# The first gate weights moved to SyncE's queue, and tile 1's statistics split around the first square root

## Chip, cores, metric

One core of a Trainium2 chip. The metric is the device time of the slowest (here the only) core in microseconds (us).

## The reference

```python
# x: (1, 2048, 512) bf16; F = 1376; all dims of the state space model are 512
xn = layernorm(x)                                     # per row, no affine part
# branch A: h[t] = Lam_bar * h[t-1] + B_bar @ xn[t]   (complex, diagonal Lam_bar)
#           y[t] = 2 * Re(C @ h[t]) + xn[t] * Dskip
# branch B: (silu(xn @ w_gate) * (xn @ w_up)) @ w_down
return x + A(xn) + B(xn)
```

## The kernel before: what matters here

x is cut into 16 tiles of 128 rows, four of them a chunk. Chunk 0 is on the path from the start: its tiles are normalized, transposed by TensorE and multiplied with the gate weights, one tile ("quarter") at a time. Later chunks are transposed by DMA. A list scheduler in the kernel orders the work of VectorE, ScalarE and GpSimd from estimated durations; TensorE's and SyncE's orders are as written.

The loads, all in SyncE's queue but two:

```python
x_load(0)
x_load(1)
act_q = [dma("ld_touch", tch[0:16, 0:1], wg_v[0:128:8, 0:1, 0:2], ..., eng="act")]   # 64 bytes
act_q.append(wg_load("a0", 0, 2, eng="act", order=(act_q[-1],)))    # gate weights, K tiles 0 and 1
x_load(2)
wg_load("a1", 2, 3)                                                 # K tile 2
wg_load("a2", 3, 4)                                                 # K tile 3
x_load(3)
pload("ld_ldt", 2, A_log_dt); pload("ld_lim", 1, A_Lambda_im); pload("ld_lre", 0, A_Lambda_re)
dma("ld_wu0", ...)      # up weights, 768 KB
dma("ld_wg1", ...)      # the other gate weights, 480 KB
dma("ld_wu1", ...)      # the other up weights, 608 KB
dma("ld_x4", ...)       # x tiles 4 to 7, 512 KB
# then, each behind all before it: transposing loads of B_re, B_im (needed by the first
# matmul of the state space branch), xT of chunk 1, x8-11, C_re, C_im, Dskip, x12-15, ...
```

VectorE's order for tiles 0 to 3 ("b": statistics of half a tile, "B": of a whole one, "s": aggregate, after which ScalarE takes the square root, "r": reciprocal, "n": normalize):

```python
last = ln_stat0(0, (bn_full(0),))
for op, a, h in (("r", 0, 0), ("n", 0, 0), ("B", 1, 0), ("s", 1, 0), ("b", 2, 0),
                 ("r", 1, 0), ("n", 1, 0), ("n", 1, 1), ("b", 2, 1), ("s", 2, 0), ...
```

Of the kernel before, what the change touches and what calls it, by code (L numbers as in the profile page):

```python
# [249 lines left out]
def bass_parallel_sum__ssm_conv_s5__swiglu_ffn__prompt_kernel(  # L250
# [30 lines left out]
    g = _Graph()  # L281
    es = ExitStack()
    with es:
        block = es.enter_context(nc.Block(no_gpsimd_drain=True))

        def sb(name, shape, dt):
            return es.enter_context(nc.sbuf_tensor(name, shape, dt))
# [39 lines left out]
        mv = sb("mv", [128, NT, 2], F32)  # L327
# [5 lines left out]
        st0 = st[:].rearrange("p (a h) s -> p a h s", h=2)  # L333
# [62 lines left out]
        def dma(name, dst, src, writes, nbytes, reads=(), after=(), out_=False, eng="sp", xpose=False, prio=0.0, order=(), **kw):  # L396
            after = tuple(after)
            if xpose:
                after = after + tuple(dma_tasks)
                fn = lambda e, dst=dst, src=src: e.dma_start_transpose(out=dst, in_=src)  # L400
                est, nb = 1900.0, int(nbytes * 1.2) + 140000
            else:
                if xp_state[0] is not None:
                    after = after + (xp_state[0],)
                fn = lambda e, dst=dst, src=src: e.dma_start(dst, src, **kw)  # L405
                est, nb = 330.0 + nbytes / 900.0, nbytes
            t = g.add(eng, fn, reads=reads, writes=writes, name=name, dma=True, after=after, out=out_, est=est, nbytes=nb, prio=prio, order=order)
            dma_tasks.append(t)
            if xpose:
                xp_state[0] = t  # L410
            return t
# [9 lines left out]
        def x_load(a, **kw):  # L421
            return dma("ld_x%d" % a, x_sb[:, a:a + 1, :], x_v[:, a:a + 1, :], [("x", a)], TILEB, **kw)

        def wg_load(nm, k0, k1, **kw):
            return dma("ld_wg" + nm, wg[:, k0:k1, 0:FG], wg_v[:, k0:k1, 0:FG], [("wg", nm)], (k1 - k0) * 128 * FG * 2, **kw)
# [2 lines left out]
        x_load(0)  # L428
        x_load(1)
        act_q = [dma("ld_touch", tch[0:16, 0:1], wg_v[0:128:8, 0:1, 0:2], [("tch",)], 16 * 4, eng="act")]  # L430
        act_q.append(wg_load("a0", 0, 2, eng="act", order=(act_q[-1],)))
        x_load(2)
        wg_load("a1", 2, 3)
        wg_load("a2", 3, 4)
# [13 lines left out]
        def loads_stage_b2():  # L448
# [11 lines left out]
              reads=[("dsk",)], writes=[("ident",)], name="ident", est=300)  # L460
        g.add("pool", lambda e: e.iota(iot[:], pattern=[[1, TP]], base=0, channel_multiplier=0, allow_small_or_imprecise_dtypes=True),
              writes=[("iot",)], name="iota", est=1000)
# [49 lines left out]
        def bn_half(a, h, order=()):  # L512
            return g.add("dve", lambda e: e.bn_stats(out=st0[:, a, h, :], in_=x_sb[:, a, h * 256:(h + 1) * 256]),
                         reads=[("x", a)], writes=[("st0", a, h)], name="bnst%d_%d" % (a, h), est=350, order=order)

        def ln_half(a, h, order=()):
            cs = slice(0, 384) if a == 0 else slice(h * 256, (h + 1) * 256)
            return g.add("dve", lambda e: e.tensor_scalar(out=xn_sb[:, a % NXN, cs], in0=x_sb[:, a, cs], scalar1=mv[:, a, 0:1], scalar2=rstd[:, a:a + 1],
                                                        op0=ALU.subtract, op1=ALU.mult),
                         reads=[("x", a), ("mv", a), ("rstd", a)], writes=[("xh", a, h)], name="xn%d_%d" % (a, h), est=300, order=order)  # L520

        def ln_stat0(a, order):
            t = g.add("dve", lambda e: e.bn_aggr(out=mv[:, a, :], in_=st0[:, a].rearrange("p h s -> p (h s)")[:, 0:6 if a < 2 else 12]),
                      reads=[("st0", a, h) for h in range(1 if a < 2 else 2)], writes=[("mv", a)], name="bnag%d" % a, est=160, order=order)
            hold["sd%d" % a] = g.add("act", lambda e: e.activation(out=sd0[:, a:a + 1], in_=mv[:, a, 1:2], func=AF.Sqrt, bias=epst[:, 0:1]),
                                     reads=[("mv", a), ("epst",)], writes=[("sd0", a)], name="sd%d" % a, est=280)
            return t

        def ln_chunk0():
            def bn_full(a, order=()):  # L530
                return g.add("dve", lambda e: e.bn_stats(out=st0[:, a, 0, :], in_=x_sb[:, a, :]), reads=[("x", a)], writes=[("st0", a, 0)], name="bnst%d" % a, est=640, order=order)
            def recip(a, order):
                return g.add("dve", lambda e: e.reciprocal(out=rstd[:, a:a + 1], in_=sd0[:, a:a + 1]), reads=[("sd0", a)], writes=[("rstd", a)],
                             name="rstd%d" % a, est=140, order=order)
            last = ln_stat0(0, (bn_full(0),))
            g.add("act", lambda e: e.activation(out=nm0[:, 0:1], in_=mv[:, 0, 0:1], func=AF.Identity, scale=-1.0), reads=[("mv", 0)], writes=[("nm0", 0)],
                  name="negm0", est=220, order=(hold["sd0"],))
            hold["negm0"] = g.tasks[-1]
            for op, a, h in (("r", 0, 0), ("n", 0, 0), ("B", 1, 0), ("s", 1, 0), ("b", 2, 0),
                             ("r", 1, 0), ("n", 1, 0), ("n", 1, 1), ("b", 2, 1), ("s", 2, 0), ("b", 3, 0),  # L540
                             ("r", 2, 0), ("n", 2, 0), ("n", 2, 1), ("b", 3, 1), ("s", 3, 0), ("p", 0, 0),
                             ("r", 3, 0), ("n", 3, 0), ("n", 3, 1)):
                if op == "r":
                    last = recip(a, (last,))
                    if a == 0:
                        g.add("act", lambda e: e.activation(out=nm0[:, 1:2], in_=nm0[:, 0:1], func=AF.Identity, scale=rstd[:, 0:1]),
                              reads=[("nm0", 0), ("rstd", 0)], writes=[("nm0", 1)], name="nmr0", est=290)
                        hold["nmr0"] = g.tasks[-1]
                        g.add("act", lambda e: e.activation(out=xn_sb[:, 0, 384:512], in_=x_sb[:, 0, 384:512], func=AF.Identity, bias=nm0[:, 1:2], scale=rstd[:, 0:1]),
                              reads=[("x", 0), ("rstd", 0), ("nm0", 1)], writes=[("xh", 0, 1)], name="xn0_1", est=400)  # L550
                        hold["xa01"] = g.tasks[-1]
                elif op == "n":
                    last = ln_half(a, h, (last,))
                elif op == "b":
                    last = bn_half(a, h, (last,))
                elif op == "B":
                    last = bn_full(a, (last,))
                elif op == "p":
                    last = g.add("dve", lambda e: e.transpose(out=prT[:], in_=prow[:]), reads=[("prow", k) for k in range(3)] + [("prow0",)],
                                 writes=[("praw", k) for k in range(3)], name="parT", est=90, order=(last,))  # L560
                else:
                    last = ln_stat0(a, (last,))
            hold["xn3"] = last
# [220 lines left out]
        def ffn_gate_quarters(pairs):  # L784
# [5 lines left out]
            pe_warm(9, 512, wbank)  # L790
            pe_warm(2, 128, wbank)
            ln_chunk0()
            xt_tile_fine(0, 0, wbank)
            pe_warm(1, 256, tiles[-2][1])
# [305 lines left out]
```

## Time and profile before

| | before |
|---|---|
| time, median of the first 3 runs | 178.72 us (178.62 to 178.73) |
| profiled execution | 179.2 us, span 177.4 us |
| TensorE busy | 173.9 us (98% of the span) |
| VectorE, ScalarE busy | 92%, 49% |

In lines of the profile, PE is TensorE, PEld its weight loads, DVE VectorE, ACT ScalarE, POOL GpSimd; SPq and ACTq are the issuing of DMAs by SyncE and ScalarE. L405 is a line of the kernel, x14 the number of instructions merged into the line, and times are in us. A K tile is 128 of the 512 rows of a weight matrix; xT is a transposed x.

The chain that ended last, by engines, from the page of before:

```profile
PE 62%; DMA 19%; DVE 7%; ACT 4%; SPq 3%; POOL 1%; issue 1%; ACTq 0%
```

A kernel whose TensorE is busy 98% has a last chain that runs through DMAs for its first third. So two chains are nearly level there.

SyncE's issues in the timeline of before (start, duration, what). The load of K tiles 0 and 1 is not here: ScalarE issued it at 1.23.

```profile
0.79 1.34 SPq L405 DMA_DIRECT2D x_sb<-in_A_x_dram  x3
2.18 0.91 SPq L405 DMA_DIRECT2D wg<-in_B_w_gate_dram  x2
3.13 0.43 SPq L405 DMA_DIRECT2D x_sb<-in_A_x_dram  x1
...
5.52 0.44 SPq L405 DMA_DIRECT2D wu<-in_B_w_up_dram  x1
...
7.10 0.82 SPq L405 DMA_DIRECT2D x_sb<-in_A_x_dram  x1
16.58 2.02 SPq L400 DMA_TRANSPOSE BT<-in_A_B_re_dram  x1
20.78 1.78 SPq L400 DMA_TRANSPOSE BT<-in_A_B_im_dram  x1
24.77 2.86 SPq L400 DMA_TRANSPOSE xnT<-xn_sb  x1
```

A transposing load is issued when all before it have landed. So the last three lines also tell landings: x4-7 by 16.58, B_re by 20.78, B_im by 24.77 (the landing records have 16.28, 20.77 and 24.70).

VectorE's first work in the timeline of before. In brackets is idle time and what ended it.

```profile
3.67 0.18 DVE L523 BATCH_NORM_AGGREGATE mv<-st 128x2 f32<-128x6 f32 x1
4.21 0.16 DVE L533 RECIPROCAL rstd<-sd 128x1 f32<-128x1 f32 x1 [0.36 <-ACT sd L525]
4.41 0.38 DVE L518 TENSOR_SCALAR xn_sb<-x_sb,mv,rstd 128x384 bf16<-128x384 bf16 x1
4.71 0.69 DVE L531 BATCH_NORM_STATS2 st<-x_sb 128x6 f32<-128x512 bf16 x1
5.43 0.18 DVE L523 BATCH_NORM_AGGREGATE mv<-st 128x2 f32<-128x6 f32 x1
5.53 0.40 DVE L513 BATCH_NORM_STATS2 st<-x_sb 128x6 f32<-128x256 bf16 x1
5.97 0.16 DVE L533 RECIPROCAL rstd<-sd 128x1 f32<-128x1 f32 x1
```

TensorE's weight loads before: in the first stage, and at the first matmuls of the state space branch.

```profile
5.50 0.79 PEld L806 LDWEIGHTS pb<-xnT,wg 128*128 128x128 bf16 x14
6.55 0.18 PEld L806 LDWEIGHTS pb<-xnT,wg 128*128 128x128 bf16 x3 [0.26 <-issue]
...
23.73 0.74 PEld L883 LDWEIGHTS pb<-xnT,BT 128*128 128x128 bf16 x4
24.75 0.16 PEld L883 LDWEIGHTS pb<-xnT,BT 128*128 128x128 bf16 x2 [0.27 <-DMA BT<-in_A_B_im_dram]
```

The 0.26 us is read as the wait for K tile 2 (landed 6.45, 0.10 before the gap ends; the profile prints only "issue"). The 0.27 us before the load at 24.75 costs nearly nothing, since weight loads run ahead of the matmuls.

Two matmul lines before: the first 512-wide one, which ends the first stage, and the wait for the last transposed x.

```profile
12.72 1.03 PE L762 MATMUL pb<-xnT,wg 128*128 128x512 bf16 x4
...
64.85 1.04 PE L845 MATMUL pb<-xnT,wg 128*128 128x512 bf16 x4 [0.17 <-DMA xnT<-xn_sb]
```

What the DMAs did meanwhile, in two-microsecond windows of before (length; busy time and count of TensorE, its weight loads, VectorE, ScalarE and GpSimd; granted clock, DMA share, GB/s):

```profile
2.00:4.00 2.00, 2.00 (x6) 0.73 (x5) 0.88 (x2) 1.40 (x3) 0.15 (x3) 1.00 0.98 296
6.00:8.00 2.00, 1.88 (x35) 1.74 (x33) 1.85 (x8) 0.94 (x5) 0.00 (x0) 1.00 0.85 164
14.00:16.00 2.00, 2.00 (x11) 0.92 (x10) 0.00 (x0) 2.00 (x4) 0.00 (x0) 1.00 0.12 35
```

### The profile page before, as it was taken

How to read it: one execution, taken by the hardware profiler on the slowest of the kernel's cores; microseconds unless marked ns; L12 is line 12 of the kernel's file. 1: busy time of each engine (PE TensorE's matmuls, PEld its weight loads, DVE VectorE, ACT ScalarE, POOL GpSimd, SP SyncE). 2: the span in 40 equal slices, each digit the busy share in tenths (PEclk: the TensorE clock that was granted, in tenths of full speed). 3: DMA queues.
4: the chain of work that ended last, by engine and by line, in shares of the span. 5: the costliest groups of instructions: out<-in, count | busy, mean ns of one | idle time of the engine just before them, and what ended most of it. 6: DMA issues, size and time to landing. Idle time of an engine off the chain costs nothing.

```text
span 177.4 us, 2425 instructions
## 1 busy us (share of the span) xinstructions
PE 173.9 (98%) x935; PEld 83.8 (47%) x935; DVE 162.5 (92%) x283; ACT 86.9 (49%) x116; POOL 11.1 (6%) x22
## 2 busy tenths in 40 slices
PE   8999999999999999999999999999999999999994
PEld 2894444444444434444444444444444444444644
DVE  2964999899899999999999999999999999999943
ACT  4679889979978869240456554000265520000000
POOL 3040500050050000000000000000000000000000
PEclk9999999999999999999999999999999999999999
DMA  5992595563468150001100000001100000000032
GB/s 169 268 373 68 120 148 95 161 133 82 134 133 283 29 102 0 0 4 66 54 0 0 0 0 4 0 0 59 59 0 4 0 0 0 0 0 30 32 110 67
DMA packets 22966, 12.37 MB, mean 70 GB/s; under 512 B 15180, under 2 KB 22956, under 8 KB 22956
## 3 DMA queue, kind: packets, MB, share of 16 engines
q1 hardware_dynamic: 22652, 11.77, 24.9%
q10 hardware_dynamic: 304, 0.46, 0.8%
q8 instruction: 7, 0.11, 0.3%
q14 instruction: 3, 0.02, 0.0%
HBM read 6.46 MB, written 2.10 MB: 48 GB/s over the span
## 4 chain that ended last, share of the span: by engine, by line
PE 62%; DMA 19%; DVE 7%; ACT 4%; SPq 3%; POOL 1%; issue 1%; ACTq 0%
PE pb L966 20%; PE pb L762 19%; PE pb L980 16%; DMA x_sb<-in_A_x_dram 7%; DMA xnT<-xn_sb 5%; PE pb L883 4%; SPq L405 3%; DVE st L483 3%; DMA hss<-in_A_C_im_dram 3%; DMA hss<-in_A_C_re_dram 2%; DMA dsk<-in_A_Dskip_dram 2%; PE pb L977 2%; ACT xn_sb L507 2%; DVE hT L834 1%; PE pb L855 1%
## 5 line engine op out<-in xcount | busy, mean ns | idle before, releaser
L923 DVE TENSOR_TENSOR_SCAN rot<-sm,car,rot 128x512 bf16<-128x512 f32 x32 | 38.8, 1266 | 0.0
L774 ACT ACTIVATE sg<-pb 128x1024 bf16<-128x1024 f32 x20 | 20.1, 1023 | 32.1 <-PE pb L762 31.3
L966 PE MATMUL pb<-wd,hT 128*128 128x512 bf16 (+2 forms) x180 | 35.2, 355 | 0.0
L980 PE MATMUL pb<-W,hss 128*128 128x512 bf16 (+2 forms) x144 | 30.3, 355 | 0.0
L762 PE MATMUL pb<-xnT,wu 128*128 128x512 bf16 x120 | 27.9, 379 | 0.0
L966 PEld LDWEIGHTS pb<-wd,hT 128*128 128x128 bf16 x180 | 16.8, 98 | 18.2 <-ACT scrC L730 0.4
L832 ACT ACTIVATE uf<-pb 128x1024 bf16<-128x1024 f32 x20 | 20.5, 1024 | 8.9 <-PE pb L762 7.3
L762 PE MATMUL pb<-xnT,wg 128*128 128x512 bf16 x92 | 21.8, 379 | 0.0
L883 PE MATMUL pb<-xnT,BT 128*128 128x512 bf16 x96 | 21.0, 379 | 0.0
L980 PEld LDWEIGHTS pb<-W,hss 128*128 128x128 bf16 x144 | 13.5, 97 | 14.4
L762 PEld LDWEIGHTS pb<-xnT,wu 128*128 128x128 bf16 x120 | 11.7, 98 | 14.2 <-ACT sg L774 0.2
L890 ACT ACTIVATE u_sb<-pb 128x1024 bf16<-128x1024 f32 x16 | 16.0, 1022 | 3.3 <-PE pb L883 3.3
L883 PEld LDWEIGHTS pb<-xnT,BT 128*128 128x128 bf16 x96 | 9.3, 98 | 11.4 <-DMA BT<-in_A_B_im_dram 0.3
L985 DVE TENSOR_TENSOR x_sb<-pb,x_sb 128x512 bf16<-128x512 f32 (+2 forms) x18 | 11.1, 628 | 3.3 <-PE pb L980 3.0
L762 PEld LDWEIGHTS pb<-xnT,wg 128*128 128x128 bf16 x92 | 9.0, 98 | 10.6
L834 DVE TENSOR_TENSOR hT<-sg,uf 128x1024 bf16<-128x1024 bf16 x20 | 13.4, 681 | 0.4 <-ACT uf L832 0.4
L483 DVE BATCH_NORM_STATS2 st<-x_sb 128x6 f32<-128x512 bf16 x12 | 7.4, 679 | 3.1 <-DMA x_sb<-in_A_x_dram 3.1
L914 DVE TENSOR_TENSOR rot<-u_sb,cosT 128x2048 bf16<-128x2048 bf16 x8 | 9.7, 1218 | 0.0
L914 DVE TENSOR_TENSOR rot<-rot,sin 128x2048 bf16<-128x2048 bf16 x8 | 9.7, 1218 | 0.0
L914 DVE TENSOR_TENSOR rot<-u_sb,sin 128x2048 bf16<-128x2048 bf16 x8 | 9.7, 1218 | 0.0
L914 DVE TENSOR_TENSOR rot<-rot,cosT 128x2048 bf16<-128x2048 bf16 x8 | 9.7, 1213 | 0.0
L914 DVE TENSOR_TENSOR rot<-rot 128x2048 bf16<-128x2048 bf16 x8 | 9.6, 1218 | 0.0
(93 smaller groups left out, 180.4 us busy)
## 6 DMA issues: line engine op xcount, KB each, us to landing
out_dram<-x_sb SPq DMA_DIRECT2D x15, 128.0 KB, 1.7
x_sb<-in_A_x_dram SPq DMA_DIRECT2D x3, 512.0 KB, 4.7
wd<-in_B_w_down_dram SPq DMA_DIRECT2D x1, 1280.0 KB, 8.6
wu<-in_B_w_up_dram SPq DMA_DIRECT2D x1, 768.0 KB, 5.0
wu<-in_B_w_up_dram SPq DMA_DIRECT2D x1, 608.0 KB, 7.0
x_sb<-in_A_x_dram SPq DMA_DIRECT2D x4, 128.0 KB, 3.2
wg<-in_B_w_gate_dram SPq DMA_DIRECT2D x1, 480.0 KB, 5.9
wg<-in_B_w_gate_dram ACTq DMA_DIRECT2D x1, 448.0 KB, 3.8
```

Source lines behind the costliest of these rows:

```text
L483: return g.add("dve", lambda e, a=a: e.bn_stats(out=st[:, a % 8, :], in_=x_sb[:, a, :]), reads=[("x", a)], writes=[("st", a % 8), ("st0", ...
L762: inst = e.matmul(pbank[0:fs, bk, :].rearrange("p (j t) -> p j t", j=4), lhsT=w[:, kt, i * 128:i * 128 + fs], rhs=xnT[c][:, :, kt, :], sta ...
L774: g.add("act", lambda e: e.activation(out=sg[rows, sl, 0:n, :].rearrange("p a t -> p (a t)"), in_=pair_f32(rows, bk, 512 * n), func=AF.Sil ...
L832: g.add("act", lambda e: e.activation(out=uf[rows, ul, 0:n, :].rearrange("p a t -> p (a t)"), in_=pair_f32(rows, bk, 512 * n), func=AF.Ide ...
L834: g.add("dve", lambda e: e.tensor_tensor(out=hT[rows, hb, i0:i0 + n, :], in0=sg[rows, sl, 0:n, :], in1=uf[rows, ul, 0:n, :], op=ALU.mult), ...
L883: inst = e.matmul(pbank[:, bk, :].rearrange("p (j t) -> p j t", j=4), lhsT=BT[:, ri, kt, pt * 128:(pt + 1) * 128], rhs=xnT[c][:, :, kt, :] ...
L890: g.add("act", lambda e: e.activation(out=u_sb[:, us].rearrange("p r t -> p (r t)"), in_=pair_f32(slice(0, 128), b0), func=AF.Identity), r ...
L914: tt = lambda out, a, b, op, r, w, nm: g.add("dve", lambda e: e.tensor_tensor(out=out, in0=a, in1=b, op=op), reads=r, writes=w, name="%s_% ...
L923: g.add("dve", lambda e, A0=A0, A1=A1, k=k, ri=ri, pt=pt: e.tensor_tensor_scan(out=A1[:, k, ri, :], data0=rr[:, pt:pt + 1].to_broadcast([1 ...
L966: inst = e.matmul(pbank[:, bk, 0:nc_], lhsT=hT[0:fs, hb, i, lt * 128:(lt + 1) * 128], rhs=wd[0:fs, i, c0:c0 + nc_], start=(i == 0), stop=F ...
L980: inst = e.matmul(pbank[:, bk, 0:nc_], lhsT=hss[:, hb, pt, ri, lt * 128:(lt + 1) * 128], rhs=W12[:, ri, pt, c0:c0 + nc_], start=False, sto ...
L985: g.add("dve", lambda e, bk=bk, a=a, c0=c0, nc_=nc_: e.tensor_tensor(out=x_sb[:, a, c0:c0 + nc_], in0=pbank[:, bk, 0:nc_], in1=x_sb[:, a, ...
```

## The change

The intent: in one queue the first loads land in the order of need (x0, x1, gate weights, x2, ...), and VectorE uses the 0.36 us in which it waits for the first square root to read half of tile 1.

```diff
         act_q = [dma("ld_touch", ...)]
-        act_q.append(wg_load("a0", 0, 2, eng="act", order=(act_q[-1],)))
+        wg_load("a0", 0, 2)
         x_load(2)
 ...
-            t = ... bn_aggr(... [:, 0:6 if a < 2 else 12]),  reads=[("st0", a, h) for h in range(1 if a < 2 else 2)]
+            t = ... bn_aggr(... [:, 0:6 if a == 0 else 12]), reads=[("st0", a, 0), ("st0", a, 1)]
 ...
-            for op, a, h in (("r", 0, 0), ("n", 0, 0), ("B", 1, 0), ("s", 1, 0), ("b", 2, 0),
+            for op, a, h in (("b", 1, 0), ("r", 0, 0), ("n", 0, 0), ("b", 1, 1), ("s", 1, 0), ("b", 2, 0),
```

A third part isn't in the diff: the scheduler, given other estimates, puts the work on the sine and cosine tables (from 17 us on) in another order on VectorE and ScalarE.

More of the change, by code (lines that the diff above doesn't have):

```diff
@@ L522, in ln_stat0 @@
         def ln_stat0(a, order):
-            t = g.add("dve", lambda e: e.bn_aggr(out=mv[:, a, :], in_=st0[:, a].rearrange("p h s -> p (h s)")[:, 0:6 if a < 2 else 12]),
-                      reads=[("st0", a, h) for h in range(1 if a < 2 else 2)], writes=[("mv", a)], name="bnag%d" % a, est=160, order=order)
+            t = g.add("dve", lambda e: e.bn_aggr(out=mv[:, a, :], in_=st0[:, a].rearrange("p h s -> p (h s)")[:, 0:6 if a == 0 else 12]),
+                      reads=[("st0", a, 0), ("st0", a, 1)], writes=[("mv", a)], name="bnag%d" % a, est=160, order=order)
             hold["sd%d" % a] = g.add("act", lambda e: e.activation(out=sd0[:, a:a + 1], in_=mv[:, a, 1:2], func=AF.Sqrt, bias=epst[:, 0:1]),
@@ L555, in ln_chunk0 @@
                     last = bn_half(a, h, (last,))
-                elif op == "B":
-                    last = bn_full(a, (last,))
                 elif op == "p":
```

## The prediction

> What bounds the kernel now. The page's first part shows TensorE busy 173.9 of 177.4 us; the timeline shows it without a real gap from its first useful matmul (5.52 us) on, except 0.26 us in its weight loads at 6.3 us (the landing times say why: the gate weights of K tile 2 landed at 6.45) and 0.17 us at 64.7 us, waiting for tile-chunk 3's transposed x. The chain of waits names a second limit: SyncE issues its first loads (about 0.47 us each, to 7.10 us), x4-7 land at 16.28, then DMA transposes and loads each wait for the one before: B_re 16.58 to 20.77, B_im to 24.70, xT, x8, C_re, C_im, Dskip, ..., the last xT at 64.81, which releases TensorE for its last 110 us. B_im's landing at 24.70 also ends a 0.27 us weight-load wait just as TensorE needs it. So both chains are level, and a gain counts only if both have it.
>
> What the change does. (1) The 448 KB of gate weights leave ScalarE's queue (issue 1.23, landed 5.03) and become SyncE's third load. The Trainium skill, "DMA: Bandwidth & Descriptors", section "Issuing engines are not separate DMA queues", says that issuing from several engines saves only the sequencer's issue time. Here that time is the point: every later SyncE load is issued about 0.47 us later (wu0 at 5.99, not 5.52; x4-7 at 7.57). (2) In one queue the early loads land in order of need: I expect x1 by about 3.5 (was 4.09), the first gate weights about 4.5 to 4.8 (5.03), K tile 2 under 6.2 (6.45). (3) VectorE reads tile 1's first half (0.40 us) in the idle 0.36 us before the first reciprocal. The reciprocal stays near 4.21; tile 1's aggregate goes from 5.43 to about 5.2, its square root from 5.65 to about 5.5. (4) VectorE's and ScalarE's table work is reordered by the list scheduler; TensorE's order is unchanged.
>
> Costs. TensorE's start (5.5) waits for the evacuation of tile 0's transposes, not for weights, and stays. It loses the 0.26 us gap, and tile 1 is early enough to follow: about 0.25 us gained by 12.7 us (first 512-wide matmul about 12.45). Against that: before, the data of the first loads ended at 6.4 us and the first 1536-byte packets of wu0 started at 6.62, with the DMA engines 3 to 7 of 16 busy in between; so wu0 is bound by its issue there. Issued 0.47 later, wu0, wg1, wu1 and x4-7 land 0.3 to 0.5 later: x4-7 about 16.7, B_re about 21.2, B_im about 25.1. TensorE reaches B_im early, waits, and is about 0.4 us later than before from there on; the last xT lands about 65.2. The reordered table work has slack (PSUM pairs come free over 3 us before their next use).
>
> Predicted 179.1 us, 8 in 10 within 178.6 to 179.5. Chance of faster by over 2%: 0.01; within 2%: 0.98; slower: 0.01.
>
> What would show it: step 1, SyncE's issue times; step 2, landings; step 3, the gap at 6.3 gone, first 512-wide matmul near 12.45; the cost, wu0's first packets near 7.1, x4-7 landing near 16.7, B_im near 25.1, a longer weight-load wait there, last xT near 65.2.
>
> What would make it wrong: wu0's slow first microsecond (6.6 to 8.2) has another cause than its issue and does not move, so that x4-7 land at 16.3 and the time is 178.6 or less; the DMA engine that lands last for x4-7 (1.3 us after the other 15; a 16 KB packet of the instruction queue held one for 0.96 us) falls otherwise; or the reordering makes TensorE wait.

## The result

| | before | changed |
|---|---|---|
| median us, beside each other | 178.76 (178.62 to 179.18, 6 runs) | 179.16 (178.84 to 179.6, 6 runs) |
| ratio, 95% interval | | 1.0019 (1.0003 to 1.0035) |
| span of the profiled execution | 177.4 us | 177.1 us |

A ratio is the mean time of one kernel's fast runs over that of the other's of the same rounds, so not quite the ratio of the medians quoted.

The predicted 179.1 us is met. But the trace at hand is of the fastest of the six executions, and that of before is of one as slow as the slowest of the six beside it (179.2), so the two traces differ the other way round: the changed kernel's span is the shorter. Reading the difference from this pair would be a mistake; what they do show are the steps.

The chain that ended last, from the page of the changed kernel. It is TensorE's alone now:

```profile
PE 96%; ACT 2%; issue 1%; DVE 0%
```

SyncE's issues, changed:

```profile
0.79 0.87 SPq L405 DMA_DIRECT2D x_sb<-in_A_x_dram  x2
1.71 0.43 SPq L405 DMA_DIRECT2D wg<-in_B_w_gate_dram  x1
2.18 0.47 SPq L405 DMA_DIRECT2D x_sb<-in_A_x_dram  x1
...
6.02 0.45 SPq L405 DMA_DIRECT2D wu<-in_B_w_up_dram  x1
...
7.60 0.96 SPq L405 DMA_DIRECT2D x_sb<-in_A_x_dram  x1
16.32 2.00 SPq L400 DMA_TRANSPOSE BT<-in_A_B_re_dram  x1
20.50 1.85 SPq L400 DMA_TRANSPOSE BT<-in_A_B_im_dram  x1
24.69 3.00 SPq L400 DMA_TRANSPOSE xnT<-xn_sb  x1
```

All from wu0 on is issued 0.50 us later. In this execution x4-7 land at the same time all the same. Their last DMA engine is probably the one that also fetched a 16 KB packet of the instruction queue (0.96 us long before, 1.11 here): that is read from the times, since the trace does not number the engines. It lands 1.3 us after the other fifteen before (14.94 and 16.28), and 1.0 us here (15.22 and 16.25). The fifteen are 0.28 later.

VectorE, changed:

```profile
3.62 0.18 DVE L523 BATCH_NORM_AGGREGATE mv<-st 128x2 f32<-128x6 f32 x1
3.71 0.40 DVE L513 BATCH_NORM_STATS2 st<-x_sb 128x6 f32<-128x256 bf16 x1
4.16 0.17 DVE L533 RECIPROCAL rstd<-sd 128x1 f32<-128x1 f32 x1
...
5.11 0.21 DVE L523 BATCH_NORM_AGGREGATE mv<-st 128x2 f32<-128x12 f32 x1
5.67 0.43 DVE L513 BATCH_NORM_STATS2 st<-x_sb 128x6 f32<-128x256 bf16 x1 [0.36 <-DMA x_sb<-in_A_x_dram]
6.02 0.15 DVE L533 RECIPROCAL rstd<-sd 128x1 f32<-128x1 f32 x1
```

The half tile fits into the wait, and the aggregate comes 0.32 us earlier (5.11, was 5.43). Then VectorE, which works in order, waits 0.36 us for x2, and the second reciprocal comes at 6.02, later than before (5.97). x2 stands behind 448 KB of weights now: issued at 2.18 in place of 1.71, landed at 5.65 in place of 5.34.

TensorE's weight loads, changed:

```profile
5.62 1.11 PEld L804 LDWEIGHTS pb<-xnT,wg 128*128 128x128 bf16 x17
...
23.74 0.74 PEld L881 LDWEIGHTS pb<-xnT,BT 128*128 128x128 bf16 x4
24.66 0.26 PEld L881 LDWEIGHTS pb<-xnT,BT 128*128 128x128 bf16 x2 [0.17 <-DMA BT<-in_A_B_im_dram]
```

The 0.26 us gap is gone in this execution, as predicted (K tile 2 landed at 6.24), but the seventeen loads start 0.12 us later and end at the same time.

The two matmul lines, changed: the first stage ends where it did, and the wait for the last transposed x is gone in this execution.

```profile
12.73 1.03 PE L760 MATMUL pb<-xnT,wg 128*128 128x512 bf16 x4
...
64.53 1.03 PE L843 MATMUL pb<-xnT,wg 128*128 128x512 bf16 x4
```

The same windows, changed. DMAs move less in the first two windows shown (in the second, the gap between the first loads and wu0 is wider) and have more left over after 14 us:

```profile
2.00:4.00 2.00, 2.00 (x6) 0.74 (x5) 1.08 (x3) 0.97 (x3) 0.15 (x3) 1.00 0.91 233
6.00:8.00 2.00, 2.00 (x40) 2.00 (x38) 1.85 (x9) 0.94 (x5) 0.00 (x0) 1.00 0.63 134
14.00:16.00 2.00, 2.00 (x11) 0.91 (x10) 0.00 (x0) 2.00 (x3) 0.21 (x1) 1.00 0.30 95
```

### The profile page after: what moved, and what is told of

Same layout as the page of the kernel before. It is cut to its first block, busy times and chain, and to the rows that moved or that the text cites. A ratio compares the mean times of both kernels' runs of the same rounds, so it can differ in the third digit from the quotient of the medians.

```text
span 177.1 us, 2420 instructions
## 1 busy us (share of the span) xinstructions
PE 173.4 (98%) x927; PEld 84.2 (48%) x935; DVE 162.6 (92%) x284; ACT 87.1 (49%) x116; POOL 11.1 (6%) x22
## 3 DMA queue, kind: packets, MB, share of 16 engines
HBM read 6.46 MB, written 2.10 MB: 48 GB/s over the span
## 4 chain that ended last, share of the span: by engine, by line
PE 96%; ACT 2%; issue 1%; DVE 0%
PE pb L760 36%; PE pb L964 19%; PE pb L881 16%; PE pb L978 16%; PE pb L804 4%; PE pb L478 3%; PE pb L975 2%; PE pb L843 1%; ACT sg L863 1%; PE pb L583 1%; ACT uf L865 1%; ACT uf L868 0%; DVE x_sb L983 0%
## 5 line engine op out<-in xcount | busy, mean ns | idle before, releaser
L964 PE MATMUL pb<-wd,hT 128*128 128x512 bf16 (+2 forms) x176 | 34.5, 355 | 0.3 <-ACT uf L868 0.2
L978 PE MATMUL pb<-W,hss 128*128 128x512 bf16 (+2 forms) x140 | 29.6, 354 | 0.2
```

The costliest lines, as they stand in the source:

```text
L964: inst = e.matmul(pbank[:, bk, 0:nc_], lhsT=hT[0:fs, hb, i, lt * 128:(lt + 1) * 128], rhs=wd[0:fs, i, c0:c0 + nc_], start=(i == 0), stop=F ...
L978: inst = e.matmul(pbank[:, bk, 0:nc_], lhsT=hss[:, hb, pt, ri, lt * 128:(lt + 1) * 128], rhs=W12[:, ri, pt, c0:c0 + nc_], start=False, sto ...
```

## The experiments

Three theories:

1. Theory 1: every later SyncE load is issued 0.5 us later; that reaches x4-7, B_re and B_im, and TensorE waits for B_im.
2. Theory 2: the reordered table work costs the time.
3. Theory 3: nothing of the change reaches the end; what differs is chance, such as when TensorE's clock warms up.

All kernels below gave correct results. All times are medians of 5 or 6 runs against 9 to 11 of before on the same chip; the twelve kernels ran on three chips. By the traces q_keep, s_only, b_slot2 and b_tw keep before's order of the table work, and r_only and a_tw that of the changed kernel; in a_act, a_pool, b_pool and a_tw_d the scheduler made yet other orders.

### q_keep: the queue alone

The statistics stay, and the order of the table work is held at that of before by moving the load only after scheduling:

```diff
         streams = _schedule(g.tasks, engs)
+        a0 = [t for t in g.tasks if t.name == "ld_wga0"][0]
+        streams[a0.eng].remove(a0); a0.eng = "sp"; streams["sp"].insert(2, a0)
```

> Only the queue of the first gate weights is changed (SyncE's third load); statistics and the order of the table work stay as before. Theory 1 (every later SyncE load is issued about 0.47 us later, and that reaches B_im and TensorE): wu0 issued at 5.99 to 6.02, x4-7 landing 0.3 to 0.5 later in most runs, time 0.3 to 0.5 us over before. Theory 2 (the reordered table work on VectorE and ScalarE costs the time): as before within 0.1. Theory 3 (no shift reaches the end; the difference is the clock's warm-up falling differently from run to run): as before within 0.2, with the same spread.

Measured: 179.20 against 178.95 us, ratio 1.0011 (0.9999 to 1.0023). wu0 was issued at 6.03 and landed at 10.77 (10.47 before), x4-7 at 16.63, B_im at 25.16. Weight loads of the state space branch:

```profile
25.20 1.41 PEld L883 LDWEIGHTS pb<-xnT,BT 128*128 128x128 bf16 x8 [0.72 <-DMA BT<-in_A_B_im_dram]
```

This is the trace that theory 1 describes, at 0.25 us in the medians; the interval just touches 1.

### r_only: the order of the table work alone

The graph of the queue-only kernel is scheduled, then the load goes back to ScalarE:

```diff
         wg_load("a0", 0, 2)                       # as changed, for the scheduler
 ...
+        streams["sp"].remove(a0); a0.eng = "act"; streams["act"].insert(1, a0)   # after _schedule
```

> Only the order of the table work on VectorE and ScalarE is that of the changed kernel; queues, loads and statistics are those of before. Theory 1: as before within 0.15 us. Theory 2: 0.3 to 0.4 us slower than before. Theory 3: as before within 0.2.

Measured: 178.80 against 178.95 us, ratio 0.9993 (0.9981 to 1.0005). Theory 2 falls. B_im landed at 24.48, and TensorE did not wait for it at all:

```profile
23.65 2.90 PEld L883 LDWEIGHTS pb<-xnT,BT 128*128 128x128 bf16 x14
```

### s_only: the statistics alone

```diff
-        wg_load("a0", 0, 2)                       # from the changed kernel
+        act_q.append(wg_load("a0", 0, 2, eng="act", order=(act_q[-1],)))
```

> Only tile 1's statistics are changed (two halves, the first in the wait for the square root); queues and table order of before. Theory 1: as before within 0.15 us; tile 1's aggregate moves from 5.43 to about 5.2 if x1 has landed by 3.8, otherwise the first reciprocal is late by the wait for x1 (x1 landed at 4.09 before, so I expect VectorE to stall about 0.3 us there, tile 0 to be about 0.3 us late, and the time up to 0.3 us over before where B_im does not hide it). Theories 2 and 3: as before within 0.1 and 0.2.

Measured: 179.09 against 178.95 us, ratio 1.0003 (0.9990 to 1.0016). VectorE:

```profile
4.41 0.43 DVE L513 BATCH_NORM_STATS2 st<-x_sb 128x6 f32<-128x256 bf16 x1 [0.66 <-DMA x_sb<-in_A_x_dram]
4.75 0.14 DVE L533 RECIPROCAL rstd<-sd 128x1 f32<-128x1 f32 x1
```

As expected: without the queue's new order x1 lands at 4.38 and holds up tile 0 itself. The first stage ended at 13.04 in place of 12.72. So the statistics need the queue move (x1 landed at 3.36 with it), and the queue move brings x2 late, which takes the gain back.

### b_slot2: only the issue of the later loads delayed, twice as much

```diff
+        for k in range(2):     # 64 bytes each; scheduled at no cost, all orders as before
+            dma("ld_slot%d" % k, tch2[:, k:k + 1], wg_v[0:128:8, 0:1, 0:2], [("tch2", k)], 0)
         dma("ld_wu0", ...)
```

> Before, plus two 64-byte loads in SyncE's queue just before wu0, scheduled at no cost so that all orders stay as before: only the issue of wu0, wg1, wu1 and x4-7 moves, by about 0.9 us. Theory 1: wu0's first packets near 7.5 (were 6.62), x4-7 landing 0.6 to 0.9 later, B_im near 25.4, a wait for it of about 0.7 to 1.0 us, time 0.6 to 0.9 us over before. Theories 2 and 3: as before within 0.2. If the landing of x4-7 is held by the DMA engine with the 16 KB instruction packet and not by the issue, x4-7 land less than 0.4 later and the time rises by less than 0.4.

Measured: 179.74 against 178.95 us, ratio 1.0047 (1.0034 to 1.0060). wu0 was issued at 6.46, its first packets ran at 7.55, x4-7 landed at 16.99 and B_im at 26.09:

```profile
26.13 0.55 PEld L887 LDWEIGHTS pb<-xnT,BT 128*128 128x128 bf16 x4 [1.73 <-DMA BT<-in_A_B_im_dram]
```

The trace is of the slowest of its six executions (180.27). In the medians 0.94 us of later issue costs 0.79 us, as theory 1 has it. Theory 3 falls as a theory of everything: issue time behind x3 reaches the end, whatever the clock does.

### An account of the span

From these traces the span comes out as a sum: the start of the first 512-wide matmul, plus 161.8 us from there to the last matmul's start if TensorE waits for nothing (r_only: 174.43 − 12.64 = 161.79), plus waits, plus 2.6 us. The waits are what is left of the last matmul's start after the first two terms; wherever that is over 0.1 us, the profile names a gap of TensorE or of its weight loads for it.

| trace | first 512-wide | B_im landed | waits |
|---|---|---|---|
| before | 12.72 | 24.70 | 0.33, for the last transposed x |
| r_only | 12.64 | 24.48 | 0 |
| s_only | 13.04 | 24.65 | 0 |
| b_tw (below) | 12.76 | 24.11 | 0 |
| changed | 12.73 | 24.62 | 0 |
| changed, after2 (below) | 12.65 | 24.90 | 0.22, B_im |
| changed, after3 (below) | 12.83 | 25.42 | 0.56, B_im |
| q_keep | 12.73 | 25.16 | 0.40, B_im |
| a_tw (below) | 13.07 | 24.86 | 0 |
| a_tw_d (below) | 12.91 | 24.99 | 0.04, B_im |

The first four have the first gate weights in ScalarE's queue, the others in SyncE's. Means of the four against the six: x4-7 landed at 15.95 and 16.49, B_im at 24.49 and 24.99. So about 0.5 us, as much as the loads are issued later, does arrive at B_im on average; it is single executions that hide it (one trace of each kernel, and the two ranges overlap, 24.11 to 24.70 and 24.62 to 25.42).

The table holds one thing more. In its four traces with a wait for B_im, and in a_act's (0.12), the wait is B_im's landing, less the start of the first 512-wide matmul, less 12.03 us. By that, before had 0.05 us of slack at B_im, r_only 0.19, s_only 0.42 and b_tw 0.67: 0.33 on average, which pays for part of the 0.5, and the mean wait of the six is 0.20 us. It also says that where TensorE waits for B_im, a shorter first stage would only have lengthened the wait (worked out, not run).

### after2 and after3: the changed kernel again

> The changed kernel once more, for a second interval and a second trace. Theory 1 (the later issue of wu0 reaches B_im and TensorE): 0.2 to 0.5 us over before; B_im lands after 24.9 in this trace unless x4-7's last engine is early again (in the first trace x4-7 landed at 16.25, B_im at 24.62, and the time was the lowest of its six). Theory 3 (chance of the clock's warm-up): as before within 0.1. If the weight loads are at the fast rate before 5.5 us, the first 512-wide matmul starts near 12.5; at the slow rate until 5.9, as in the first trace, near 12.7.

> The changed kernel a third time, beside the same runs of before as the three below. From the traces so far a run's span is the start of the first 512-wide matmul + 161.8 us + the waits for B_im and for the last transposed x + 2.6 us. Theory 1: first 512-wide matmul at 12.6 to 12.75 as before (x2 lands near 5.65 and VectorE waits for it, which takes back the early statistics), B_im at 24.6 to 25.2 (before: 24.5 to 24.7), wait 0 to 0.4 us, time 0.0 to 0.4 over before. Theory 3: as before within 0.1.

Measured: 179.11 against 179.22 us, ratio 0.9990 (0.9974 to 1.0007), and 179.05 against 179.13 us, ratio 1.0004 (0.9990 to 1.0018). So the first interval's 0.19% did not come again. The three ratios average to 1.0004, which is under 0.1 us: no difference that these runs can tell from none. The later landing is in the traces all the same. In after3 the weight loads of the state space branch:

```profile
25.46 1.19 PEld L881 LDWEIGHTS pb<-xnT,BT 128*128 128x128 bf16 x7 [0.88 <-DMA BT<-in_A_B_im_dram]
```

and in after2 VectorE waited for x2 as in the first trace:

```profile
5.71 0.43 DVE L513 BATCH_NORM_STATS2 st<-x_sb 128x6 f32<-128x256 bf16 x1 [0.39 <-DMA x_sb<-in_A_x_dram]
```

My expectation for after2's first stage was a miss: weight loads were fast from 4.46 on, and it still ended at 12.65, not near 12.5. The clock's warm-up alone does not explain the missing gain. The two traces show where it went. In after2 the weight loads lost about 0.07 us to K tile 2 (landed 6.30) and 0.16 to tile 1: those of its transposes came at 6.64, 0.58 us after the second reciprocal (6.06), the same 0.58 to 0.60 as in r_only, q_keep, a_act, a_pool and a_tw, where TensorE also waited for tile 1. In after3 K tile 2 landed at 6.56, later than before's 6.45, and the gap that the change should close was there again:

```profile
6.60 0.17 PEld L804 LDWEIGHTS pb<-xnT,wg 128*128 128x128 bf16 x3 [0.28 <-DMA wg<-in_B_w_gate_dram]
```

### a_act: the issue slot paid back

```diff
-        pload("ld_lre", 0, A_Lambda_re)
 ...
         act_table(AF.Sqrt, (act_q[-1],))
+        pload("ld_lre", 0, A_Lambda_re, eng="act", order=(g.tasks[-1],))
```

> The changed kernel with one of the three small parameter loads moved from SyncE's queue to ScalarE's, after its table is warm, so that wu0 is issued about 0.55 us earlier (5.45), where before had it. Theory 1: the slot is paid back: x4-7 and B_im land as before or 0.1 earlier, time as before or up to 0.2 under it, and 0.3 to 0.5 under the changed kernel. Theory 3: like the changed kernel within 0.1. If the small load on ScalarE's queue takes longer than about 0.9 us there, the first square root is late and tile 0 with it.

Measured: 179.09 against 179.22 us, ratio 0.9995 (0.9976 to 1.0014), beside after2's 0.9990: no difference. The issue came back to 5.53, but wu0 landed at 10.68, as late as with the change, and B_im at 24.98. A miss: in this execution the loads ahead of wu0 were themselves late (K tile 2 at 6.47, x3 at 7.38), and wu0's first packets came at 6.82, 0.20 later than before's. Issue time is one bound on wu0 (b_slot2); the data ahead of it in the queue seems to be another, close behind. So it is not shown that the change's 0.5 us come by the issue slot alone.

### a_pool and b_pool: the small parameter loads in GpSimd's queue

In the changed kernel and in before, the three small loads leave SyncE's queue:

```diff
-        pload("ld_ldt", 2, A_log_dt); pload("ld_lim", ...); pload("ld_lre", ...)
 ...
+        pool_setup = tuple(t for t in g.tasks if t.eng == "pool")
+        pload("ld_ldt", 2, A_log_dt, eng="pool", order=pool_setup)   # and the other two
```

> The changed kernel with all three small parameter loads on GpSimd's queue, after its constants. wu0 is issued near 4.1 and its packets follow x3's without the gap at 6.4 to 7.1. Theory 1: wu0, wg1, wu1 and x4-7 land 0.5 to 1.0 earlier than before, B_im near 23.8 to 24.2, no wait for it; TensorE alone is then the limit, and the 0.25 us of the first stage counts: 0.2 to 0.6 us under before. Theory 3: as before within 0.2.

> Before, with all three small parameter loads on GpSimd's queue: B_im early as in a_pool, but the first stage as before. Theory 1: B_im near 23.8 to 24.2, time 0.0 to 0.3 under before, and 0.1 to 0.3 over a_pool, which is what the queue order and the early statistics are worth once nothing hides them. Theory 3: as before within 0.2, no difference between a_pool and this.

Measured: a_pool 179.77 against 179.22 us, ratio 1.0037 (1.0003 to 1.0072); b_pool 179.58, ratio 1.0019 (1.0002 to 1.0036). Half of the expectation held. B_im landed at 23.67 and 24.19, and TensorE did not wait for it in either. But both are slower. In a_pool x2 landed at 6.11 and x3 at 8.26, and VectorE waited for both. The first gate weights landed only at 5.82, so the first stage began 0.43 us later (5.93, was 5.50), and it ended 0.75 us later than before:

```profile
6.13 0.43 DVE L515 BATCH_NORM_STATS2 st<-x_sb 128x6 f32<-128x256 bf16 x1 [0.70 <-DMA x_sb<-in_A_x_dram]
...
8.28 0.43 DVE L515 BATCH_NORM_STATS2 st<-x_sb 128x6 f32<-128x256 bf16 x1 [0.44 <-DMA x_sb<-in_A_x_dram]
```

```profile
13.47 1.03 PE L762 MATMUL pb<-xnT,wg 128*128 128x512 bf16 x4
```

With B_im out of the way that reaches the end one to one: 13.47 + 161.79 + 2.57 = 177.83, the span of this trace. b_pool's loss is another one, a wait for ScalarE's table work (waits of 0.70 us in all). That work is in another order there; that the order is the cause is likely, but was not tested:

```profile
57.63 5.35 PE L885 MATMUL pb<-scrC,BT 128*128 128x512 bf16 x24 [0.54 <-ACT uf L834]
```

Why x2 and x3 land late in a_pool, though they stand before wu0 in the same queue, was not tested.

### a_tw, a_tw_d and b_tw: is wu0's slow start its first access?

wu0's packets start slowly: in the changed kernel's first trace 27 of 1536 bytes ran in the 0.8 us from 7.0, against some 50 in each 0.2 us from 8.6. The kernel's first load, 64 bytes of the gate weights, looks like a remedy for such a start; so the same was tried for the up weights, in the changed kernel (a_tw) and in before (b_tw), and in a_tw_d VectorE also takes tile 2's first half after tile 1 is normalized:

```diff
+        act_q.append(dma("ld_touch2", tch[0:16, 1:2], wu_v[0:128:8, 0:1, 0:2], ..., eng="act", ...))
# a_tw_d also:
-   ("b", 1, 1), ("s", 1, 0), ("b", 2, 0), ("r", 1, 0), ("n", 1, 0), ("n", 1, 1), ("b", 2, 1),
+   ("b", 1, 1), ("s", 1, 0), ("r", 1, 0), ("n", 1, 0), ("n", 1, 1), ("b", 2, 0), ("b", 2, 1),
```

> The changed kernel plus a second 64-byte load on ScalarE's queue that reads the up weights' tensor before wu0 does (as the kernel's first load already does for the gate weights); the orders of all engines stay those of the changed kernel. If wu0's slow first 0.8 to 1.2 us is the first access to its tensor, wu0's packets run at full rate (near 50 in 0.2 us) from 7.1 on, wu0 lands near 10.0, x4-7 near 15.6 and B_im near 24.1: no wait for B_im, time 0.2 to 0.4 under the changed kernel. If the slow start has another cause, landings and time stay as in the changed kernel within 0.15.

> As the run with the second touching load, and VectorE takes tile 2's first half after tile 1's normalization, not before its reciprocal, so that it doesn't wait there for x2 (0.36 to 0.39 us in the traces of the changed kernel). Theory 1: second reciprocal near 5.85 (was 6.02 to 6.06), first 512-wide matmul near 12.5 (was 12.65 to 12.73); with B_im out of the way the 0.1 to 0.2 us reach the end. If B_im still lands near 24.9, they do not.

> Before, plus the second touching load on ScalarE's queue behind the gate weights. If the slow start is the first access: B_im near 23.7, no waits, time 0.0 to 0.3 under before (before's B_im hardly costs anything; the wait for the last transposed x, 0.3 us in its first trace, goes). Otherwise as before within 0.15.

Measured, against 179.13 us: a_tw 179.16, ratio 1.0005 (0.9991 to 1.0018); a_tw_d 179.10, ratio 1.0004 (0.9992 to 1.0017); b_tw 178.84, ratio 0.9988 (0.9974 to 1.0001). The slow start stayed: a_tw's counts from 7.0 were 7, 12, 9 and 15 in each 0.2 us (43 in all; the three traces of the changed kernel have 27, 29 and 45), and wu0 landed at 10.72. So the slow start is not cured by an earlier access of this form; its cause is open. a_tw_d is a miss as well: the second reciprocal came at 5.97, but the third at 8.04 (7.74 in the first trace), and the first stage ended at 12.91. No version was shown to beat both kernels; b_tw has the lowest ratio, and its interval holds 1.

## Why the prediction was right, and where not

**The time: right.** 179.1 predicted, 179.16 measured beside before's 178.76. Two further sets of rounds give 179.11 and 179.05 us, still in the range, but before then has 179.22 and 179.13. So the level was met, while the difference of 0.4 us, which the text argues, is under 0.1 us on average: its size was wrong. The hit is partly luck: the range of 178.6 to 179.5 holds all four medians of before as well, so a forecast of no change would have been as right, and the first set's 0.4 us did not come again.

**Step "every later SyncE load is issued about 0.47 us later": right.** 0.50 us (wu0 at 6.02, x4-7 at 7.60). The Trainium skill calls the sequencer's time for an issue "usually small relative to the DMA itself" ("DMA: Bandwidth & Descriptors", section "Issuing engines are not separate DMA queues"). Here an issue takes 0.43 us and a 128 KB load at before's 296 GB/s (estimate: 0.44 us) no longer, and b_slot2 shows that two more issues cost 0.79 us.

**Step "in one queue the early loads land in order of need": right in order, partly wrong in size.** x1 landed at 3.36 (predicted 3.5). The first gate weights landed at 5.32, later than from ScalarE's queue (5.03), not at 4.5 to 4.8; K tile 2 at 6.24, just over the 6.2, in the first trace. Over the ten traces of the table K tile 2 came no earlier at all: 6.41 on average, against 6.35 with the old queue (6.23 to 6.45). The first gate weights came 0.27 us later (5.41, 5.14), and so did x2 (5.74, 5.47). The windows show that my figure was too good, and not why: from 2 to 4 us the DMAs moved 233 GB/s, not 296, though their busy share fell only from 0.98 to 0.91.

**Step "x4-7 and B_im land 0.3 to 0.5 later": right on average** (0.54 and 0.50 between the means above), and not in the first trace.

**Step "TensorE ... is about 0.4 us later than before from there on": the mis-sized term.** I took B_im as landing "just as TensorE needs it", from one trace. That trace has the latest B_im of the four with the old queue and only 0.05 us of slack there; the four have 0.33 on average. So the 0.5 us cost 0.20 us on average in six traces, between 0 and 0.56. The other wait of before's trace, 0.33 us for the last transposed x, was special to it too: r_only, s_only and b_tw do not have it. The chain that "ended last" in one trace was one of two level chains.

**Step "about 0.25 us gained by 12.7 us": failed.** The first stage ended at 12.65 to 12.83 in the three traces of the changed kernel. The gap of 0.26 us was itself special to before's trace: r_only, s_only and b_tw, with the old queue, do not have it, and after3, with the new one, does. The aggregate came at 5.11 to 5.12. But the text takes tile 1 to be early from that alone; it has no figure for x2, which now stands behind 448 KB. VectorE waited 0.36 and 0.39 us for it in two of the traces, and the second reciprocal did not come near 5.8 but at 6.02 and 6.06. In the third x2 landed at 5.55 and the reciprocal came at 5.92, but K tile 2 landed at 6.56, and the stage ended no earlier. Over the three traces the second reciprocal came at 6.00 on average, against 6.02 in before, r_only and b_tw.

In the first trace TensorE's clock has a part: its weight loads took up to 152 ns until 5.81 (147 until 4.63 before) and 98 ns from 5.92. The clock is read from these durations alone; the granted clock of the windows is 1.00 in both. The Trainium skill, "TensorE: Matmul & The Clock Gate", Part 1, puts the moment of warm-up down to a free-running window of activity and calls it run-variable. The traces agree that it varies: over the fourteen, the first weight load under 100 ns after the start came between 3.7 and 6.3 us, and in the three of the changed kernel at 5.92, 4.46 and 4.01. That looks like chance, not the change.

**Step "the reordered table work has slack": right** (r_only).

What stays open: why one queue brings the first gate weights and x2 later than two did, how much of the 0.5 us is issue time and how much the data ahead, and why wu0 starts slowly.

## What to carry to other kernels

Before you read a slack or a gap of a few tenths of a microsecond from a trace, look at it in several executions: the landing of one DMA moved by 0.6 us between four traces of kernels with the same SyncE queue, and the gap of 0.26 us that this change was to close was in one of the four. When a consumer far down a queue has little slack, issue slots at its head can reach it (0.79 us for two, b_slot2); count them against what the reordering brings. And an engine that works in order gains nothing by finishing one input's work early if its next instruction waits for a load that the same change made later.

## What the Trainium skill lacked or had wrong

- "DMA: Bandwidth & Descriptors", section "Issuing engines are not separate DMA queues": it says that another issuing engine saves only issue time, which is usually small. It lacks the case in which that time decides: 0.43 us for each issue of SyncE, and 0.79 us of kernel time for two more of them ahead of wu0 (b_slot2).
- The same page has no word on a slow start of a large load: wu0's 1536-byte packets ran at about a seventh to a fifth of their later rate for 0.8 us (27, 29 and 45 in three traces of the changed kernel, against some 50 in each 0.2 us later), and no faster after an earlier 64-byte access to the tensor (43, a_tw).
- "Runtime: NRT & Kernel Launch", section "Instruction fetch mechanics", says that instructions come in 16 KiB blocks and calls the cost of crossing into the next one mostly hidden. It does not say what the fetch does to other loads. A 16384-byte packet of the instruction queue was on a DMA engine for 0.96 us (before) and 1.11 us (changed), and x4-7's last engine landed 1.3 and 1.0 us after the other fifteen; one at 53.2 us in before took 2.63 us. That the one caused the other is read from the times, not tested. "DMA: Bandwidth & Descriptors", section "Queues, rings and completion order", has the refill in row 14; the profile of before has seven of these packets in queue 8, and three smaller packets of the instruction kind in queue 14; whether it counts queues as the page counts rows is not shown.
- "TensorE: Matmul & The Clock Gate", Part 1, gives a variation of plus or minus 500 ns for the moment of warm-up. Over these fourteen traces, taken as the first weight load under 100 ns, it lay between 3.7 and 6.3 us (the first matmul starts at 0.83), and in three traces of one kernel between 4.01 and 5.92.
